# A gated linear attention and a feed-forward layer on one core: wider products of zeros, and another order, engines and banks

## The chip, the cores and the metric

The kernel runs on one core of one Trainium2 chip. The metric is the device time of one execution in microseconds (us); lower is better. A core has five engines, each with its own queue of instructions that it works off in order: TensorE (PE in the profile; its weight loads are shown as PEld), VectorE (DVE), ScalarE (ACT), GpSimd (POOL) and SyncE (SP), which here only issues DMAs. Engines wait for each other by semaphores. TensorE writes its results to eight banks of PSUM; GpSimd does not read these in this kernel.

## What is computed

Per batch and head, a state of 48 x 48 decays and takes in one outer product per time step; a query reads it. The rows that come out, for all heads side by side (384 columns, 3,072 rows), go through two matrix products with a squared ReLU between them.

```python
batch, n_heads, seq, head_dim = (4, 8, 768, 48)
n_tokens, d_model, d_ff = (3072, 384, 2048)
for t in range(S):
    state = alpha[:, :, t, :, None] * state + einsum('bhd,bhe->bhde', k[:, :, t], v[:, :, t])
    y[:, :, t] = einsum('bhd,bhde->bhe', q[:, :, t], state)
h = x @ w_in            # x: y with the heads side by side
r = maximum(h, 0.0)
out = (s * (r * r) + b) @ w_out
```

## The kernel before

The time axis is cut into chunks of 128 steps: 6 chunks for each of 4 batches, 24 blocks in all. Inside a block the recurrence becomes products. The names below are those of the list `ORDER`; the number behind a name is the block, the group or the piece.

- Loads on SP: `pa0` to `pv2` load alpha, q, k, v for two blocks at a time for the first six blocks (384 KB each), `a6` to `v23` for one block (192 KB). `i0` to `i3` load quarters of `w_in` and `o0` to `o3` quarters of `w_out` (768 KB each).
- `ln` (L324, ScalarE) takes the logarithm of alpha, `cum` (L335, L348 to L361, TensorE) sums it along time, `eb`, `ei`, `el` (L368, L373, L381, L386, ScalarE) take exponentials of the sums. `qb` and `kb` (L234, VectorE or GpSimd) multiply q and k by them. `vc` copies v.
- `T` and `Tc` transpose q and k on TensorE and copy the result (the first six blocks); `Td` (L426) does it with a DMA from SP (the others). `A` (L481, L491) gives the scores, `mk` (L502, L508, VectorE) masks them. `KV` (L439, L451), `t` (L464, L466) and `sn` carry the state from block to block. `y`, `ya`, `ys` (L530, L544, L561) give the block's output, transposed, and `ye` copies it to `xd`.
- `m` (L592) is one of 96 pieces of the first matrix product: six products of 256 columns, two blocks at a time (a group of eight `m`). `re` (L599 on ScalarE, L601 on VectorE) is the ReLU out of a bank, `sq` (L609 on ScalarE, L234 on VectorE) the square.
- `w` (L626) is a quarter of the second matrix product for one block: four products of 384 columns. The last block is done in two halves of columns (`w92` to `w95`, L618, eight products of 192). `oe` (L641, L636) adds the bias and scales, `st` (L654, L649) stores.
- `ci`, `co` convert the weights to bf16 on three engines; `ca` to `cd`, `bm`, `be` make the bias row from `w_out`.
- `z` (L659) are products of zeros whose result nobody reads. `FILLS` gives each its bank, the number of products and their width.

There is no loop over the work: `ORDER` is a list written out in full, and L738 to L740 emit it word by word. Each engine gets its instructions in the order in which they stand in it. A prefix (`A:`, `D:`, `P:`) sets another engine than the usual one (`DEF`). The lists `T_BANK`, `C_BANK`, `A_BANK`, `KV_BANK`, `Y_BANK`, `O_BANK`, `H_BANK` name the PSUM bank of each result, and `R_BANK` which of four buffers a ReLU writes. Whoever writes a bank next waits until the last user's result has been read.

Of the kernel before, what the change touches and what calls it, by code (L numbers as in the profile page):

```python
# [29 lines left out]
SB_BANK, BIAS_BANK = 2, 6  # L30
T_BANK = {0: 3, 1: 1, 2: 1, 3: 3, 4: 6, 5: 4}
C_BANK = [0, 4, 6, 5, 4, 5, 2, 2, 5, 1, 4, 4, 7, 6, 0, 1, 2, 5, 7, 4, 0, 5, 2, 3]
A_BANK = [2, 1, 1, 6, 2, 2, 4, 2, 3, 6, 3, 2, 4, 6, 0, 5, 1, 4, 4, 1, 3, 6, 1, 6]
KV_BANK = [5, 0, 0, 3, 5, 0, 2, 3, 2, 0, 6, 0, 0, 7, 5, 2, 1, 0, 7, 3, 2, 4, 4, 0]
Y_BANK = [6, 4, 0, 6, 2, 7, 5, 2, 0, 6, 1, 3, 2, 7, 6, 7, 4, 5, 2, 7, 0, 5, 5, 4]
O_BANK = [0, 3, 4, 7, 0, 6, 1, 5, 1, 3, 4, 3, 6, 3, 0, 6, 6, 3, 3, 5, 4, 7, 5, 2, 1]
# [15 lines left out]
qb2 T1 KV1 pq2 pk2 KV0 P:kb3 zvp3 A:Tc1 el2 z4 A1 ya0 P:kb2 vc2 t0 mk1 t1 z5 T3 ys1 ya1 ln4 ln5 T2
cum5 i3 Tc3 A:vc3 ye1 KV3 KV2 ye0 Tc2 sn1 A3 cum4 eb5 A2 t2 el5 ei5 mk3 ci0 P:ci1 zs2 pv2 i1 ys2
el4 eb4 ei4 sn2 m0 m1 mk2 ys3 t3 P:ci5 re1 ya3 ya2 D:ci4 re0 sq0 qb5 ye3 ye2 m5 qb4 m4 m8 m9 P:ci7
o0 re5 re4 a6 A:sq4 A:sq5 kb5 sq1 re8 T5 kb4 m13 re13 T4 Tc5 ci6 A:sq13 m12 A5 D:re9 Tc4 D:of0 mk5
m7 sn3 m6 A:sq8 vc5 m15 s0 D:vc4 D:re12 A:sq9 o3 A4 re6 re7 ci2 KV5 KV4 m14 mk4 ci3 A:sq12 o1 o2
re15 m2 ya5 a8 a7 a9 k7 k6 A:sq15 ya4 ys4 t4 D:sn4 ys5 q6 D:co1 D:re14 P:co0 D:re2 D:ye4 v6 m10 m3
w0 w8 sm0 sq7 ln6 q7 v7 k8 sq6 A:sq14 re3 ye5 re10 U0 m21 m16 A:sq10 m11 re21 A:sq21 co7 sq2 sq3
ca0 se0 D:re16 P:co6 cum6 D:co3 el6 re11 A:sq11 ei6 ca3 sq16 m23 m18 w12 m17 m19 re18 ln8 D:re23
D:co2 re19 eb6 re17 ln7 ca1 D:co5 w4 D:co4 cb0 w9 m20 ca2 cb1 kb6 sq17 A:sq18 w13 A:sq19 cc0 qb6  # L60
cd0 D:re20 a11 a10 m22 cum8 w10 w1 cum7 w5 w11 w2 ei8 el8 eb7 ln9 el7 re22 qb7 w6 w14 bm0 w3 eb8
w7 ei7 A:sq22 be0 oe0 sq23 D:vc6 A:sq20 A:vc7 Td6 P:kb7 w20 w16 KV6 w15 w21 cum9 oe2 Td7 q8 t6
ln10 ei9 ln11 oe1 oe3 eb9 w22 A6 A7 w17 w18 w23 mk6 cum10 mk7 y6 y7 q9 KV7 oe5 D:ye7 k9 v9 v8 q10
k10 w19 eb10 ei10 ye6 el10 cum11 m31 el9 t7 oe4 P:qb8 m26 P:qb9 D:re31 kb8 A:vc8 ei11 m25 m24
D:re25 D:re24 m27 A:sq25 m29 eb11 A:sq24 P:kb9 D:re26 P:qb10 k11 Td9 D:re27 D:vc9 P:kb10 A:sq31
KV8 m30 w24 q11 Td8 w28 re30 KV9 A:sq26 a12 sq30 D:re29 sn7 t8 D:sn8 A:sq27 m28 w25 re28 A:sq28
A:sq29 A9 Td10 v10 A8 w29 t9 w26 ln12 mk9 v11 a13 w27 w30 mk8 cum12 y8 y9 A10 P:kb11 w31 P:qb11
ye8 oe6 sn9 D:vc10 el12 ye9 ln13 mk10 vc11 eb12 m37 KV10 Td11 m34 oe7 m36 t10 q13 k13 cum13 k12
a15 D:re34 A11 re36 re37 mk11 m35 ei12 el13 sq36 m39 eb13 m32 sn10 re39 ei13 a14 q12 q14 y11 v13
qb13 sq39 sq37 kb12 ye11 y10 P:kb13 D:re35 ln15 ye10 D:re32 A:sq35 m38 m33 m46 cum15 D:re33 A:sq32  # L70
m44 A:sq33 a17 D:re46 ln14 D:re38 sq38 m45 m42 w36 m41 cum14 Td13 A:sq46 sq34 el15 D:re42 D:re44
ln17 m40 A:sq44 P:qb12 Td12 k14 v12 w37 re45 el14 w38 w39 ei14 eb15 ei15 D:re40 A13 D:vc13 sq45
oe9 A12 A:sq40 mk12 v14 w32 mk13 m43 w33 re41 sq41 a18 a16 w34 A:vc12 eb14 re43 P:kb14 KV12 A:sq43
v15 m47 q15 sq42 t12 w35 A:vc14 ln16 y13 y12 qb14 ye12 w44 D:ye13 re47 cum17 v19 k15 cum16 oe8 k16
eb16 A:sq47 ei17 KV13 P:qb15 m53 v16 Td14 t13 w40 m48 kb15 D:re48 eb17 ln18 el16 re53 ei16 KV14
m55 w41 m52 D:re55 m50 Td15 A:sq55 re52 m54 P:kb16 vc15 w45 KV15 m51 D:sn13 A:sq48 re54 q17 D:re50
t14 D:vc19 A14 mk14 sn14 A:sq50 A15 mk15 t15 w42 w46 A:sq52 q18 A:sq54 w47 m49 y14 re51 y15 oe11
k19 k17 P:qb17 vc16 D:re49 D:sn15 KV16 w43 q16 ye14 ye15 m59 a19 A:sq49 ln19 A:sq51 sq53 qb16 k18
a20 a21 q20 P:kb17 cum18 m57 oe10 w52 m61 Td16 re57 D:re59 Td17 m56 w53 m58 q19 v17 A:sq57 ei18
sq59 D:re61 v18 cum19 ei19 el19 el18 eb18 w54 t16 m63 re58 A:sq61 w55 m62 D:re63 D:re56 sn16 eb19  # L80
P:kb18 sq58 P:kb19 q21 a22 A16 A17 mk17 oe13 ln20 w48 w49 cum20 k20 k23 vc17 w50 m60 w51 D:re62
ei20 el20 eb20 A:sq56 mk16 re60 P:qb19 y17 y16 w56 ln21 A:vc18 a23 ye17 ln22 qb18 KV18 cum21 ye16
ei21 P:kb20 t18 KV19 w57 cum22 A:sq63 Td18 eb21 ei22 k21 m67 ln23 eb22 oe12 sq60 P:qb20 Td19 t19
sq62 m71 w60 el21 P:qb21 D:re71 D:re67 m68 m69 el22 m66 w61 A:sq71 kb21 k22 v20 D:re68 re66 w62
P:kb22 A:sq67 A18 A19 A:sq66 D:re69 cum23 w58 w63 Td20 mk19 m64 Td21 q22 sn19 y19 mk18 y18 D:ye18
eb23 ye19 w59 m65 ei23 A:vc20 v22 oe15 oe14 sq69 m72 re65 A21 A20 m70 A:sq65 P:qb22 re64 re72 mk21
mk20 vc22 v21 A:sq64 m76 re70 vc21 m79 KV20 st2 q23 st0 P:kb23 A:sq68 A:sq70 st11 Td22 st8 st3
re79 w64 t20 qb23 sq79 w65 KV21 D:sn20 t21 w66 w67 w68 m77 re76 oe16 re77 A:sq76 w69 sq72 Td23 m74
m78 D:re74 y21 sq77 re78 ye21 y20 sn21 A22 mk22 A:sq78 ye20 A23 KV22 m75 w70 m73 m86 D:re75 mk23
re86 A:sq75 w71 v23 st16 D:re73 m80 m81 st1 oe17 D:vc23 t22 m87 sq86 m85 sn22 re87 y22 y23 A:sq87  # L90
re80 ye23 A:sq80 sq73 sq74 m84 D:ye22 m82 re84 m88 D:re81 m83 A:sq81 st15 st10 re82 sq84 st4 m89
w80 re83 m94 sq82 A:sq83 m91 re85 A:sq85 re94 D:re89 w81 st7 st9 sq94 w76 m90 A:sq89 w72 m92 w77
re92 A:sq92 D:re90 D:re91 A:sq91 A:sq90 m95 w73 w78 D:re88 m93 w82 w74 w75 w79 sq88 D:re95 oe18
# [17 lines left out]
def kernel(  # L111
# [319 lines left out]
    def kv_view(n):  # L431
        return BANK[KV_BANK[n]][:, 0:384].rearrange("a (p e) -> a p e", p=NP)

# [220 lines left out]
        e.dma_start(out=out[n * C : (n + 1) * C, :], in_=out_sb[n % NOS])  # L654

    def o_z(e, x):
        bank, m, w = FILLS[x]
        for _ in range(m):
            nc.tensor.matmul(  # L659
                out=BANK[bank][:, 0:w], lhsT=zeros[:, 0:128], rhs=zeros[:, 0:w], start=True, stop=True  # L660
            )
# [109 lines left out]
```

## Time and profile before

| | us |
|---|---|
| median of 3 runs | 178.99 (178.43 to 179.17) |
| profiled execution, its own time | 179.38 |
| its span, first to last instruction | 177.7 |
| TensorE busy in the span | 169.5 |
| VectorE, ScalarE, GpSimd busy | 134.0, 111.3, 54.6 |
| first product of zeros starts | 1.25 |
| last product ends, end of the span | 174.6, 177.7 |

The durations come from the profiled execution. Its own time is 0.39 us above the median of the runs, and its span is 1.68 us shorter than its own time. Matmuls are pipelined: the duration of a single one is longer than the spacing from one to the next, so a group of products is priced by the spacing of their starts. In the timeline, a bracket behind an instruction gives the idle time of its engine just before it and what ended it; "issue" means that the profile shows no semaphore that ended it.

### The profile page before, as it was taken

How to read it: one execution, taken by the hardware profiler on the slowest of the kernel's cores; microseconds unless marked ns; L12 is line 12 of the kernel's file. 1: busy time of each engine (PE TensorE's matmuls, PEld its weight loads, DVE VectorE, ACT ScalarE, POOL GpSimd, SP SyncE). 2: the span in 40 equal slices, each digit the busy share in tenths (PEclk: the TensorE clock that was granted, in tenths of full speed). 3: DMA queues.
4: the chain of work that ended last, by engine and by line, in shares of the span. 5: the costliest groups of instructions: out<-in, count | busy, mean ns of one | idle time of the engine just before them, and what ended most of it. 6: DMA issues, size and time to landing. Idle time of an engine off the chain costs nothing.

```text
span 177.7 us, 5545 instructions
## 1 busy us (share of the span) xinstructions
PE 169.5 (95%) x2289; PEld 127.7 (72%) x2289; DVE 134.0 (75%) x239; ACT 111.3 (63%) x242; POOL 54.6 (31%) x83
## 2 busy tenths in 40 slices
...
GB/s 146 325 318 289 271 329 360 313 280 199 141 224 191 200 144 198 146 203 174 192 171 226 128 209 184 197 210 186 207 127 266 185 344 139 4 0 0 141 208 98
DMA packets 113708, 34.96 MB, mean 197 GB/s; under 512 B 106900, under 2 KB 112148, under 8 KB 113684
## 3 DMA queue, kind: packets, MB, share of 16 engines
...
q8 instruction: 18, 0.29, 0.7%
...
## 4 chain that ended last, share of the span: by engine, by line
PE 71%; DVE 7%; SPq 7%; ACT 6%; DMA 4%; issue 3%; POOL 1%; DVEq 0%; ACTq 0%
PE bank_ps L626 31%; PE bank_ps L592 28%; SPq L188 5%; DMA wst<-in_moe_w_in_dram 4%; PE bank_ps L481 3%; ACT gt L609 2%; PE bank_ps L544 2%; DVE r L601 2%; ACT r L599 2%; PE bank_ps L335 2%; PE bank_ps L530 2%; SPq L258 2%; PE bank_ps L618 1%; DVE am L502 1%; PE bank_ps L439 1%
## 5 line engine op out<-in xcount | busy, mean ns | idle before, releaser
L592 PE MATMUL bank_ps<-xd,w_in_bf 128*128 128x256 bf16 x576 | 72.0, 273 | 1.8 <-DVE r L601 1.1
L626 PE MATMUL bank_ps<-w_out_bf,gt 128*128 128x384 bf16 x368 | 68.1, 326 | 0.0
L592 PEld LDWEIGHTS <-w_in_bf 128*128 128x128 bf16 x576 | 54.5, 98 | 12.2 <-issue 0.9
L626 PEld LDWEIGHTS <-gt 128*128 128x128 bf16 x368 | 34.5, 98 | 19.5 <-issue 0.2
L599 ACT ACTIVATE r<-bank_ps 128x512 bf16<-128x512 f32 x52 | 30.6, 597 | 16.6 <-PE bank_ps L592 11.9
L609 ACT ACTIVATE gt<-r 128x512 bf16<-128x512 bf16 x61 | 36.8, 628 | 5.4 <-DVE r L601 4.9
L601 DVE TENSOR_SCALAR r<-bank_ps 128x512 bf16<-128x512 f32 x44 | 29.3, 685 | 8.9 <-PE bank_ps L592 6.4
L234 POOL TENSOR_TENSOR qk<-k_in,binv 128x384 bf16<-128x384 f32 x16 | 17.0, 1066 | 39.3 <-ACT binv L373 26.6
L502 DVE TENSOR_TENSOR am<-bank_ps,U_bf 128x1024 bf16<-128x1024 f32 x18 | 21.5, 1220 | 4.1 <-PE bank_ps L481 3.6
L234 DVE TENSOR_TENSOR gt<-r 128x512 bf16<-128x512 bf16 x35 | 17.1, 507 | 3.5 <-ACT r L599 3.3
L641 DVE SCALAR_TENSOR_TENSOR wst<-bank_ps,s_col,bias_w 128x384 f32<-128x384 f32 x23 | 14.0, 614 | 6.9 <-PE bank_ps L626 6.4
L234 POOL TENSOR_TENSOR qk<-q_in,b_s 128x384 bf16<-128x384 f32 x13 | 13.4, 1031 | 17.4 <-DMA q_in<-in_q_dram 13.9
L373 ACT ACTIVATE binv<-bank_ps 128x384 f32<-128x384 f32 x24 | 11.9, 498 | 10.3 <-PE bank_ps L342 7.7
L234 POOL TENSOR_TENSOR s_st<-t,blast 128x384 bf16<-128x384 bf16 x11 | 9.4, 855 | 23.7 <-DVE t L466 23.6
L229 ACT ACTIVATE xd<-bank_ps 128x384 bf16<-128x384 f32 x19 | 9.4, 520 | 9.8 <-PE bank_ps L544 9.2
L324 ACT ACTIVATE la<-a_in 128x384 bf16<-128x384 f32 x24 | 12.3, 522 | 5.1 <-DMA a_in<-in_alpha_dram 5.1
L368 ACT ACTIVATE b_s<-bank_ps 128x384 f32<-128x384 f32 x24 | 12.0, 499 | 4.5 <-PE bank_ps L342 3.4
L466 DVE TENSOR_TENSOR t<-bank_ps,s_st 64x192 bf16<-64x192 f32 x32 | 11.3, 352 | 1.7 <-POOL s_st L234 0.6
L234 DVE TENSOR_TENSOR qk<-q_in,b_s 128x384 bf16<-128x384 f32 x11 | 6.0, 550 | 6.3 <-DMA q_in<-in_q_dram 5.9
L659 PE MATMUL bank_ps<-zeros 128*128 128x128 bf16 x81 | 7.2, 255 | 1.3 <-DVE half_bf L695 1.3
L508 DVE TENSOR_TENSOR am<-bank_ps,maskp 128x1024 bf16<-128x1024 f32 x6 | 7.3, 1223 | 0.7 <-PE bank_ps L491 0.6
L530 PE MATMUL bank_ps<-qkT,s_st 128*32 128x128 bf16 x240 | 6.8, 221 | 0.6 <-issue 0.6
...
## 6 DMA issues: line engine op xcount, KB each, us to landing
...
```

The costliest lines, as they stand in the source:

```text
L234: e.tensor_tensor(out=o, in0=x, in1=y, op=ALU.mult)
L324: e.activation(out=la_sb[u % NLA].rearrange("a (r h) d -> a r h d", r=2)[..., 0:D], in_=seen("a", u), func=AF.Ln,)
L368: e.activation(out=b_sb[u % NB].rearrange("a h d -> a (h d)"), in_=BANK[C_BANK[u]][:, 0:384], func=AF.Exp)
L373: e.activation(out=binv_sb[u % NB].rearrange("a h d -> a (h d)"), in_=BANK[C_BANK[u]][:, 0:384], func=AF.Exp, scale=-1.0,)
L466: e.tensor_tensor(out=t1_sb[n % 2][r, :, c], in0=kv[r, :, c], in1=s_sb[(n - 1) % 3][r, :, c], op=ALU.add,)
L502: e.tensor_tensor(out=am.rearrange("a e p t -> a (e p) t"), in0=a_ps.rearrange("a e p t -> a (e p) t"), in1=U_bf.unsqueeze(1).to_broadcast ...
L592: nc.tensor.matmul(out=hp[:, i * 256 : (i + 1) * 256], lhsT=w_in_bf[:, kk, 128 * j : 128 * (j + 1)], rhs=xd_sb[g % 3][:, kk, :], start=(kk ...
L599: e.activation(out=r_sb[R_BANK[w]], in_=BANK[H_BANK[w]], func=AF.Relu)
L601: e.tensor_scalar_max(r_sb[R_BANK[w]], BANK[H_BANK[w]], 0.0)
L609: e.activation(out=o, in_=r, func=AF.Square)
L626: nc.tensor.matmul(out=BANK[bank][:, 0:d_model], lhsT=gt_sb[:, j, c0 : c0 + C], rhs=w_out_bf[:, j, :], start=(j == 0), stop=(j == NJ - 1),)
L641: e.scalar_tensor_tensor(out=out_sb[n % NOS], in0=BANK[O_BANK[n]][:, 0:d_model], scalar=s_col[:, 0:1], in1=bias_w, op0=ALU.mult, op1=ALU.add,)
```

## The change

The products of zeros are given by columns instead of by number and width, and each takes up to 512 columns. The list `ORDER`, the engines in it and all bank lists are replaced by others. The operations other than `z` are the same; the numbers of engines change thus: `re` from 52 on ScalarE and 44 on VectorE to 67 and 29; `sq` from 61 and 35 to 57 and 39; `ye` from 19 and 5 to 12 and 12; `vc` from 8 on each of ScalarE, VectorE and GpSimd to 6, 2 and 16; `ci` from 4, 1 and 3 to 4, 2 and 2; `co` from 1, 5 and 2 to 3, 4 and 1; `Tc` from 1 and 5 to 2 and 4. The diff, with the bank lists and the middle of the order cut out:

```diff
-FILLS = [(0, 32, 128), (1, 12, 128), (1, 4, 128), (1, 15, 128), (7, 12, 128), (7, 6, 128)]
+FILLS = [(0, 4288), (0, 256), (0, 1280), (0, 256), (2, 2240), (2, 960), (4, 2048), (4, 320), (3, 896)]
...
     def o_z(e, x):
-        bank, m, w = FILLS[x]
-        for _ in range(m):
+        bank, cols = FILLS[x]
+        while cols:
+            w = min(cols, 512)
             nc.tensor.matmul(
                 out=BANK[bank][:, 0:w], lhsT=zeros[:, 0:128], rhs=zeros[:, 0:w], start=True, stop=True
             )
+            cols -= w
```

The start of each engine's queue, before and after:

```
SP before: pa0 pk0 pa1 pq0 pv0 pq1 pk1 pa2 pv1 i0 i2 pq2 pk2 i3 pv2 i1 o0 a6 s0 o3 o1 o2 a8 a7 a9
SP after:  pa0 pa1 pv0 pk0 pq0 pq1 pk1 pa2 pv1 i0 i2 pk2 pq2 i3 pv2 i1 a7 s0 o0 a6 o1 o2 k7 o3 k6
TensorE before: z0 cum0 cum1 z1 cum2 cum3 z2 T0 z3 A0 T1 KV1 KV0 z4 A1 ya0 z5 T3 ys1 ya1 T2 cum5 KV3 KV2
  A3 cum4 A2 ys2 m0 m1 ys3 ya3 ya2 m5 m4 m8 m9 T5 m13 T4 m12 A5 m7 m6 m15 A4 KV5 KV4 m14 m2 ya5 ya4 ys4
TensorE after: z0 cum0 cum1 z1 cum2 z2 cum3 z3 KV1 z4 T0 T1 KV0 z5 A0 z6 T3 A1 ys1 T2 ya0 A3 ya1 KV3 KV2
  ys2 cum5 A2 cum4 m0 ya3 ya2 ys3 m4 m1 m9 m8 m12 z7 T5 m5 T4 m13 A5 A4 z8 m15 m7 m14 KV4 KV5 ya5 ya4 m6
ScalarE before: ln0 ln1 eb0 ei0 ln2 el1 ln3 ei1 el0 eb1 ei2 eb2 vc0 eb3 el3 ei3 Tc1 el2 ln4 ln5 vc3 ye1 ye0 eb5 el5 ei5 ci0
ScalarE after:  ln0 ln1 ln2 el1 ei1 ei0 ln3 eb1 el0 eb2 eb0 eb3 el3 el2 ei2 ei3 Tc1 ln5 Tc3 ln4 vc2 ye0 ye1 ci0 ci1 eb5 ei5
VectorE before: qb0 kb1 zvp0 zvp2 Tc0 vc1 mk0 qb2 t0 mk1 t1 Tc3 Tc2 t2 mk3 mk2 t3 ci4 sq0
VectorE after:  vc1 zqk2 kb1 kb0 qb0 qb1 qb2 Tc0 t0 mk0 t1 mk1 Tc2 mk3 t2 mk2 ci4 t3 ye2
```

The end of TensorE's and SP's queues:

```
TensorE before: w75 w79 w84 w83 w88 w89 w85 w86 w90 w87 w91 w92 w93 w94 w95
TensorE after:  w79 w83 w74 w87 w92 w88 w75 w89 w94 w90 w91 w93 w95
SP before: st18 st19 st12 st6 st17 st20 st14 st21 st22 st23 st24
SP after:  st16 st2 st12 st18 st21 st20 st19 st22 st23 st24
```

More of the change, by code (lines that the diff above doesn't have):

```diff
@@ L29 @@
 TAIL = 1
[L30 to L36, printed above, removed]
@@ L37 @@
-H_BANK = [5, 7, 1, 6, 6, 1, 1, 7, 3, 7, 5, 6, 0, 1, 6, 4, 3, 6, 3, 5, 1, 1, 6, 1, 0, 3, 6, 5, 4,
-7, 0, 5, 5, 0, 4, 4, 5, 0, 2, 1, 4, 2, 4, 3, 5, 6, 4, 4, 0, 0, 6, 7, 2, 1, 1, 7, 6, 2, 2, 5, 4, 4,
-7, 1, 1, 4, 5, 4, 7, 3, 0, 1, 2, 0, 0, 5, 5, 7, 4, 1, 7, 6, 3, 6, 2, 0, 2, 3, 7, 2, 2, 6, 0, 6, 3,
-2]
-R_BANK = [3, 0, 2, 1, 2, 1, 0, 3, 2, 0, 3, 1, 1, 1, 1, 2, 2, 0, 3, 1, 0, 0, 1, 2, 3, 1, 1, 3, 1,
-2, 0, 2, 0, 1, 3, 2, 2, 0, 2, 1, 1, 2, 0, 3, 3, 2, 0, 1, 0, 1, 3, 3, 1, 2, 0, 3, 2, 3, 3, 1, 3, 2,
@@ L43 @@
-1, 0, 1, 2, 2, 1, 3, 0, 0, 3, 2, 0, 3, 1, 1, 0, 1, 1, 2, 0, 2, 0, 1, 0, 2, 2, 0, 3, 1, 2, 3, 3, 1,
-1]
-FILLS = [(0, 32, 128), (1, 12, 128), (1, 4, 128), (1, 15, 128), (7, 12, 128), (7, 6, 128)]
-ORDER = """
-zz0 Us0 P:zqk0 P:zla0 pre0 pa0 Ui0 zt1 sml0 pk0 pa1 ln0 P:zla1 zs1 ln1 zqk2 zvp1 z0 cum0 eb0 ei0
-pq0 cum1 pv0 ln2 el1 ln3 pq1 ei1 pk1 mp0 D:zt0 zqk1 zs0 id0 P:kb0 pa2 qb0 kb1 zvp5 D:zvp0 z1 cum2
-el0 eb1 cum3 P:qb1 z2 T0 pv1 ei2 D:zvp2 Tc0 D:vc1 eb2 A:vc0 eb3 i0 z3 A0 P:qb3 i2 mk0 zvp4 el3 ei3
@@ L52 @@
[L52 to L93, printed above, removed]
@@ L94 @@
-w84 w83 st13 oe19 w88 re93 sq93 w89 w85 A:sq95 oe20 st5 w86 w90 w87 st18 st19 w91 st12 st6 st17
-oe21 st20 st14 oe22 st21 st22 w92 w93 oe23 st23 w94 w95 oe24 st24
+SB_BANK, BIAS_BANK = 5, 7
+T_BANK = {0: 6, 1: 3, 2: 5, 3: 6, 4: 7, 5: 1}
+C_BANK = [4, 5, 7, 1, 2, 0, 1, 3, 5, 1, 1, 3, 2, 1, 3, 5, 1, 2, 7, 1, 4, 3, 2, 4]
+A_BANK = [1, 2, 6, 6, 4, 0, 4, 2, 3, 6, 4, 2, 2, 0, 1, 5, 2, 5, 4, 0, 3, 6, 2, 6]
+KV_BANK = [0, 5, 1, 5, 3, 0, 7, 7, 1, 6, 7, 0, 1, 0, 2, 1, 0, 0, 5, 7, 5, 5, 4, 0]
+Y_BANK = [0, 4, 3, 4, 1, 5, 5, 3, 2, 3, 7, 3, 3, 0, 2, 5, 4, 3, 1, 0, 2, 5, 5, 7]
@@ new lines @@
+O_BANK = [4, 3, 0, 2, 0, 6, 0, 5, 7, 6, 4, 3, 0, 5, 6, 3, 0, 1, 3, 1, 7, 4, 0, 2, 6]
+H_BANK = [1, 5, 4, 0, 7, 2, 2, 6, 7, 0, 3, 7, 6, 6, 0, 7, 3, 6, 7, 1, 5, 7, 2, 6, 5, 1, 7, 4, 6,
+2, 0, 3, 7, 3, 0, 1, 6, 1, 5, 5, 2, 4, 1, 2, 4, 3, 6, 0, 3, 6, 5, 0, 4, 4, 6, 6, 5, 7, 7, 4, 3, 6,
+2, 2, 0, 5, 2, 7, 1, 5, 4, 4, 7, 0, 0, 2, 1, 2, 6, 0, 3, 5, 5, 4, 2, 0, 3, 2, 5, 0, 6, 3, 2, 2, 6,
+5]
+R_BANK = [2, 0, 0, 0, 0, 2, 3, 2, 2, 3, 0, 1, 1, 3, 2, 1, 2, 2, 3, 1, 0, 1, 3, 3, 2, 0, 2, 3, 3,
+0, 1, 3, 2, 1, 3, 0, 1, 0, 1, 2, 3, 3, 2, 0, 1, 0, 2, 3, 1, 1, 2, 1, 2, 3, 0, 0, 3, 2, 1, 2, 0, 1,
@@ new lines @@
+0, 3, 0, 3, 3, 1, 3, 0, 2, 1, 0, 2, 1, 2, 0, 3, 0, 3, 2, 2, 0, 2, 3, 0, 2, 1, 1, 0, 0, 0, 3, 3, 1,
+2]
+FILLS = [(0, 4288), (0, 256), (0, 1280), (0, 256), (2, 2240), (2, 960), (4, 2048), (4, 320), (3, 896)]
+ORDER = """
+zz0 zqk1 D:zvp3 D:zvp2 D:zs1 D:zs0 zvp1 Ui0 P:zqk0 P:zla1 D:zt1 zla0 pre0 of0 zvp5 sml0 D:zs2 pa0
+pa1 D:zvp0 id0 ln0 pv0 pk0 Us0 mp0 pq0 ln1 pq1 D:vc1 zqk2 z0 cum0 cum1 vc0 ln2 pk1 el1 ei1 ei0 ln3
+eb1 el0 z1 cum2 kb1 pa2 pv1 z2 cum3 z3 KV1 eb2 eb0 kb0 i0 qb0 z4 T0 qb1 qb2 Tc0 eb3 el3 el2 ei2
@@ new lines @@
+ei3 T1 KV0 i2 P:qb3 pk2 t0 z5 A0 P:kb3 mk0 A:Tc1 z6 T3 t1 ln5 A:Tc3 A1 mk1 P:kb2 vc3 ys1 zt0 sn1
+T2 ln4 ya0 A3 ya1 A:vc2 pq2 ye0 Tc2 KV3 KV2 ys2 mk3 ye1 t2 cum5 sn2 zvp4 A2 cum4 ci0 m0 ya3 i3 mk2
+ci1 eb5 D:ci4 ya2 ys3 pv2 t3 ei5 el5 ei4 D:ye2 ye3 m4 kb4 re0 re4 kb5 m1 m9 sq4 m8 eb4 qb5 m12 el4
+A:sq0 qb4 z7 T5 re1 P:ci5 i1 re8 sq8 m5 T4 P:ci6 sn3 Tc5 U0 vc5 re12 re9 A:sq9 m13 A5 Tc4 mk5 A4
+ci7 re13 z8 m15 re5 m7 mk4 sq12 A:sq5 sq13 A:vc4 re7 m14 a7 s0 KV4 o0 a6 KV5 A:sq7 re15 ci3 ya5
+re14 ya4 D:ci2 m6 m2 t4 ln7 A:sq14 D:sn4 A:sq15 m10 o1 ys5 ys4 m3 D:re6 sq1 re10 o2 D:ye4 D:ye5
@@ new lines @@
+ln6 A:sq10 m11 A:sq6 m22 m16 re16 re22 A:sq22 A:sq16 D:re11 sq11 sm0 k7 D:re3 se0 o3 P:co1 m18 m19
+sq3 D:co0 m17 D:co3 k6 re2 cum7 a8 q6 D:re19 ca0 sq2 co2 el7 re18 w12 w8 w0 cum6 a9 q7 v6 ca1 sq19
+sq18 m21 eb7 v7 a11 m20 w13 el6 D:co4 w1 ei6 co5 re17 w9 re20 eb6 re21 ei7 ca2 cb0 kb6 w14 kb7
+D:co6 qb6 m23 w4 w2 A:sq17 A:sq21 co7 Td6 a10 ca3 cb1 qb7 re23 ln8 A:sq20 cc0 ln9 w5 w20 w15 w10
+cum8 Td7 k8 A:vc7 q8 w11 cum9 k9 ln11 v8 cd0 a12 w6 q9 vc6 bm0 eb8 ei9 w7 w3 w21 be0 KV6 ln10 eb9
+el8 el9 ei8 w22 cum10 eb10 A:sq23 oe3 ei10 oe2 oe1 A7 oe0 A6 t6 w16 w17 w18 w23 mk6 mk7 y7 y6 w19
@@ new lines @@
+k10 P:kb9 P:qb8 P:kb8 KV7 ye6 P:qb9 q10 v9 q11 D:ye7 ln12 el10 m24 cum11 m27 t7 oe5 re24 ei11 m25
+oe4 m26 m28 vc8 Td8 re27 Td9 eb11 D:re25 k11 A:sq24 sq27 KV8 m29 a13 re28 m31 m30 A:sq25 D:re26
+v11 v10 sn7 re29 A:sq26 cum12 sq28 w28 P:kb10 re30 qb10 t8 re31 A:sq29 sq30 D:sn8 w29 A8 A9 eb12
+el12 ei12 w30 vc9 A:sq31 v13 ln13 P:kb11 P:qb11 vc11 vc10 w24 w25 mk8 Td10 mk9 v12 y8 y9 KV9 cum13
+ye9 w26 Td11 D:ye8 KV10 t9 w31 w27 oe7 sn9 m33 oe6 D:re33 v16 q12 t10 m36 a14 el13 ei13 eb13 k13
+m35 A10 A11 m34 A:vc13 mk10 D:re34 mk11 A:sq33 sn10 re36 re35 m32 re32 A:sq32 sq35 m37 m38 y10 q13
```

26 lines of the change are left out of this document (added).

## The prediction

> **What bounds the kernel now.** I read the page's first and fourth parts, then two stretches, then TensorE's timeline.
>
> ```profile
> PE 169.5 (95%) x2289; PEld 127.7 (72%) x2289; DVE 134.0 (75%) x239; ACT 111.3 (63%) x242; POOL 54.6 (31%) x83
> ...
> PE 71%; DVE 7%; SPq 7%; ACT 6%; DMA 4%; issue 3%; POOL 1%; DVEq 0%; ACTq 0%
> ```
>
> TensorE is busy 95% of the span and carries 71% of the chain that ended last. The chain's other shares lie where TensorE waits, mostly at the start:
>
> ```profile
> 0.00:22.08 22.08, 18.59 (x428) 15.60 (x428) 13.47 (x32) 14.58 (x37) 15.49 (x37) 1.00 0.96 270
> 22.08:177.70 155.62, 150.90 (x1862) 112.07 (x1862) 120.53 (x208) 96.76 (x207) 39.10 (x46) 1.00 0.87 186
> ```
>
> (Columns: length; busy time of PE, PEld, DVE, ACT, POOL; clock; DMA share; GB/s.) Up to 22.08 us the DMA engines are full (0.96) and TensorE waits for inputs and weights, with products of zeros between. From 22.08 to its last product at 174.55, 152.5 us, it is nearly never idle. I priced each step there by the start-to-start spacing usual for its kind (an m of six products 0.65 us, a w of four 0.65, and so on): 147.4 us. So 5.1 us are stalls, and no order can save more than that after 22.08. The large ones, in TensorE's timeline (the bracket is idle time and what ended it):
>
> ```profile
> 20.36 0.35 PE L530 MATMUL bank_ps<-qkT,s_st 128*32 128x128 bf16 x12 [0.57 <-issue]
> 20.64 0.81 PE L561 MATMUL bank_ps<-am,vp 64*32 64x128 bf16 x64
> 22.08 1.16 PE L592 MATMUL bank_ps<-xd,w_in_bf 128*128 128x256 bf16 x9 [0.62 <-POOL w_in_bf L231]
> ...
> 34.40 0.82 PE L592 MATMUL bank_ps<-xd,w_in_bf 128*128 128x256 bf16 x6 [0.74 <-DVE r L601]
> ...
> 73.02 0.41 PE L544 MATMUL bank_ps<-am,vp 128*32 128x128 bf16 x16 [0.43 <-DVE am L502]
> ...
> 82.39 0.83 PE L592 MATMUL bank_ps<-xd,w_in_bf 128*128 128x256 bf16 x6 [0.39 <-DVE r L601]
> ```
>
> Over the usual spacing the last three cost 0.91, 0.60 and 0.56 us; all three end with VectorE. The first (ys3) ends with "issue": all its semaphores had come by 19.8. I read it as missing instructions. The DMA part has the records:
>
> ```profile
> q8 instruction: 18, 0.29, 0.7%
> ```
>
> That is 16 KB, some 256 instructions, a packet (4,578 weight loads and products in 18). Their starts, 11.10, 17.90, 21.41, 29.06, 35.30, 44.66 and so on, fit requests at instructions 200, 456, 712, 968 (+256): I read that packet n+1 is asked for as packet n is entered, and must be there 256 instructions later. Instruction 456 is ya1, 14.1 us; its packet began at 17.90, after 3.8 us, ended at 18.87, and ys3, at instruction 702 to 726, ran at 20.36, 1.5 us on. The same packets delay loads: of each load's 16 landings the last is 1.3 us behind the fifteenth for pa2 and pv1 (14.00, 15.17; packet of 11.10) and 1.1 us for i2 (20.89; packet of 17.90). ScalarE pays at once:
>
> ```profile
> 14.08 0.94 ACT L324 ACTIVATE la<-a_in 128x384 bf16<-128x384 f32 x2 [2.00 <-DMA a_in<-in_alpha_dram]
> ```
>
> **The change, part by part. Wider products.**
>
> ```profile
> L659 PE MATMUL bank_ps<-zeros 128*128 128x128 bf16 x81 | 7.2, 255 | 1.3 <-DVE half_bf L695 1.3
> ```
>
> 81 products of 128 columns (10,368 columns) become 28 (12,544). z0 goes from 4,096 to 4,288 columns at 0.111 us per 128 (32 in 3.55 us): +0.17, ending at 4.97. That moves cum0, but kb0 and qb0 wait for pk0 and pq0, which now land later than that: nothing. z1 to z6 hold 7,040 columns against 6,272 in z1 to z5, at 0.056 us per 128: +0.34, all in waits for loads. z7 and z8 are new, 1,216 columns, 0.53 us, behind m12 and A4: nothing if TensorE waits there for w_in anyway, 0.53 if not. I take +0.25.
>
> **Instruction packets.** 53 products and 53 weight loads less put every later step 106 instructions earlier in the count. Counting the new order: 200 falls in z6 (was A0), 456 in KV3 (was ya1), 712 in ys3 again, 968 in ya5 (was A5); 17 packets instead of 18.
>
> **Start.** SP's order is now pa0 pa1 pv0 pk0 pq0 pq1 pk1 pa2 pv1 i0 i2: the same bytes ahead of i0, one pair per 1.21 us, so pk0 lands at 7.9 (was 5.4) and pq0 at 9.05 (was 7.9). qb0 waits for both pq0 and eb0, T0 starts near 10.0 (was 8.57): +1.4. The chain behind it: Tc0 0.69, A0 0.4, mk0 1.2, t1 0.7, mk1 1.2 on VectorE bring ya1 to 16.0 (was 14.2). If the first packet, now asked for at 12.0 to 12.9, runs behind pa2 and pv1, these land at 12.7 and 13.9, 1.3 us earlier, and ln4, ln5, vc2, vc3 with them. On ScalarE vc2, ye0, ye1, ci0 (0.63, 0.52, 0.52, 0.85) then end near 18.3, so m0 starts at 18.4 (was 18.31). There was slack: xd was ready at 16.7, and m0 waited for i0 (17.2) and ci0. ya3, ya2 and ys3 are past at 20.5; m4 waits for i2 and ci4 (0.69): 20.5 with i2 at 19.8, 21.6 with i2 at 20.9. Before, m5 came at 22.08 with m1 (0.65) already done. So 21.2 to 22.3 stands against 22.08: −0.9 to +0.2 with the packets in time, up to +3 if not (first rival). I take −0.2.
>
> **The dense stretch.** ReLU (re) moves from VectorE to ScalarE 15 times (44 to 29 by 0.685; 52 to 67 by 0.597), 7 ye and 4 sq the other way, vc to GpSimd. By the rows VectorE has about 7 us less to do, ScalarE 4 more: 127 and 116. In the old order VectorE's queue was long where the stalls are. Banks: I summed TensorE's work between one user of a bank and the next, after its first 20 us. Under 1.2 us there were 8 such returns, now 4; under 1.6 us 35, now 23. From an m to the first w that needs it, 10 were under 3.5 us, now 3. If stalls went with the 35 and 23, 5.1 would become 3.4, −1.7; if the new order only moves them, 0; several queues on ScalarE at 0.6 to 0.9 each could add 2. I take −1.2, nearer the count.
>
> **Tail.** The last five w are as dense as before. But st18, st21, st20 and st19 now follow w75, which ends 3.9 us before the last product, and st22, st23, st24 come right behind: five stores of 192 KB and two of 96 KB, 1.18 MB. Eight stores issued from 142.2 to 146.2 us ran at 344 GB/s (the page's GB/s in that slice), so 3.4 us, nearly hidden: 0 to +0.5, I take +0.1.
>
> **Sum.** 0.25 − 0.2 − 1.2 + 0.1 = −1.05. The profiled execution took 179.38 (span 177.7 and 1.68 around it): 178.33. The median, 178.99, lies 0.39 below it, so 177.9.
>
> **Rivals.**
>
> - Late packets, slower, 0.20. If the first packet waits 3.8 us, as that of 17.90 did behind 2 KB pieces of i0 and i2, it starts at 15.8 to 16.7 and serves at 18.2 to 19.1; KV3, ready near 16.2, stands 2 to 3 us, and m0 with it. The second packet, asked for only then, holds ys3 again. m4 starts at 23.5 to 24.5; with m1 undone, +2 to +3. With +0.25, −1.2 and +0.1: 180.1 to 181.1. It decides at a start after 13.7 us for the first packet (KV3's 16.2 less 0.96 and 1.5). For: the 3.8 us. Against: the packet of 11.10 waited 1.2 to 2.5 us and that of 21.41 waited 1.0; with such waits the first packet starts at 13.0 to 15.4, and the worst of that holds KV3 by 1.7 us, of which the wait for i2 behind m0 hides about 1. [...]
> - ScalarE becomes the queue, slower, 0.10. From 70 to 80 us of TensorE's work its rows sum to 11.9 us. A relu late there holds a bank as VectorE's did: three or four stalls of 0.6 to 0.9 above the old 5.1, +2.4 in place of −1.2, and hence +2.5: 181.5 at most, 180.3 with half. Against: before and after that stretch it has 5.8 and 4.4.
> - The change does not do what it says, 0.24: packets collide as before and the stalls only move. −0.2 to +0.5, 178.8 to 179.5.
> - All of it works, 0.06: the start gives −0.9 and stalls fall to 2 us (−3.1): with +0.25 and +0.1, about 175.3; half of that, 177.1.
>
> My forecast has 0.40. About 0.5% (0.9 us) is what a measurement of this kernel can tell from no change. Faster, below 178.1: 0.40 + 0.06 = 0.46; same 0.24; slower, above 179.9: 0.20 + 0.10 = 0.30. The range leaves out the best corner and the worst of the slow cases: 176.4 to 180.6; the forecast alone has 177.0 to 178.1.
>
> **What would show it.** Right: pa2 and pv1 landing near 12.7 and 13.9; no "issue" idle before KV3 or ys3; m4 at 20.5 to 21.6; above-spacing time after the start near 4 us, few "DVE r" releasers; last landing under 0.5 us later after the last product than the 3.1 of now. Wrong: "issue" idle over 1 us before KV3 or ys3, or "ACT r" as releaser of TensorE in the dense stretch for over 2 us.

## The result and the profile after

The kernel after takes 189.41 us (median of 4 runs, 188.93 to 190.72), beside 178.71 of the kernel before on the same chip: ratio 1.0608, 95% interval 1.0549 to 1.0668. It is 6.1% slower; forecast were 177.9 us, with a range to 180.6. The profiled execution took 189.42 us, its span is 187.7, ten more than before. From its page, the busy times, the chain that ended last and the queue of instruction packets:

```profile
PE 171.4 (91%) x2233; PEld 124.5 (66%) x2236; DVE 129.1 (69%) x231; ACT 115.3 (61%) x247; POOL 55.7 (30%) x86
...
q8 instruction: 17, 0.28, 0.6%
...
PE 58%; SPq 17%; DMA 12%; issue 5%; POOL 4%; DVE 2%; POOLq 0%
```

VectorE and ScalarE have nearly the work that was forecast (127 and 116). But TensorE's share of the chain falls from 71% to 58%, and the shares of SP's queue and of the DMA rise from 7 and 4 to 17 and 12. The same two stretches, up to 22.08 us and behind it, now of the kernel after and in the same columns:

```profile
0.00:22.08 22.08, 18.21 (x349) 11.49 (x352) 14.22 (x37) 13.73 (x31) 11.32 (x32) 1.00 0.99 292
22.08:187.70 165.62, 153.18 (x1884) 113.04 (x1884) 114.83 (x195) 101.59 (x216) 44.38 (x54) 1.00 0.82 172
```

Most of the loss lies behind 22.08. By the prediction's usual spacings TensorE's time above the work (products of zeros not counted as work) is 22.4 us from its first product to its last, instead of 12.5: +9.9 (the last product ends at 184.43, before at 174.55). TensorE's timeline shows where:

```profile
17.79 0.23 PE L561 MATMUL bank_ps<-am,vp 64*32 64x128 bf16 x2 [1.83 <-issue]
...
22.34 0.23 PE L561 MATMUL bank_ps<-am,vp 64*32 64x128 bf16 x2 [0.82 <-issue]
...
79.49 0.40 PE L481 MATMUL bank_ps<-qkT 64*128 64x128 bf16 x8 [0.76 <-DMA qkT<-qk]
...
93.79 0.40 PE L481 MATMUL bank_ps<-qkT 64*128 64x128 bf16 x8 [0.99 <-DMA qkT<-qk]
...
108.10 0.40 PE L481 MATMUL bank_ps<-qkT 64*128 64x128 bf16 x8 [1.23 <-DMA qkT<-qk]
...
123.73 0.49 PE L592 MATMUL bank_ps<-xd,w_in_bf 128*128 128x256 bf16 x3 [1.51 <-ACT blast L386]
...
133.35 0.40 PE L481 MATMUL bank_ps<-qkT 64*128 64x128 bf16 x8 [1.07 <-DMA qkT<-qk]
```

The first two stand just ahead of KV3 and ys3; I read them as the late instruction packets: from the one stop to the other there are 128 products with as many weight loads, 256 instructions, as the prediction counts for a packet. The others are new: A11, A12, A14 and A18 (the last line) wait for a `Td`, and A19 right behind A18 does too. Above the usual spacing A11, A12, A14, A18 and A19 cost 0.88, 1.15, 1.35, 1.24 and 1.32 us; KV14 costs 1.13 (it waits for `vc`), m59 1.62. The stalls of before that ended with VectorE are gone. The view of waits (us in all, times, longest) has GpSimd, before and then after, and SP after:

```profile
POOL vp L231 <- DMA v_in<-in_v_dram: 2.9, 3, 1.7
...
POOL vp L231 <- DMA v_in<-in_v_dram: 31.2, 6, 17.5
...
SPq L261 <- DVE w_in_bf L231: 8.2, 1, 8.2
```

GpSimd stands 31.2 us at `vc` for a late v, with the rest of its queue behind it. At m59 this is the chain: vc19 waits 9.69 us for v19; behind it stand qb19, vc17 and sn16; `el20` on ScalarE waits for sn16, and m59 writes the bank that `el20` reads. SP stands at o1 from 25.2 to 33.7 us, 8.2 us by the profile: o1 overwrites the buffer that ci2 and ci3 read, and in the new order these end at 33.4 (on VectorE, which the view names) and 33.7 (on ScalarE). In the kernel before, SP stood 3.7 us there, with o3 sent just ahead. In the kernel after the DMA engines run nearly dry meanwhile. 28 to 36 us, before and then after:

```profile
28.00:36.00 8.00, 7.26 (x156) 5.50 (x155) 7.73 (x13) 6.87 (x13) 2.28 (x4) 1.00 1.04 329
```

```profile
28.00:36.00 8.00, 7.84 (x179) 6.31 (x178) 7.42 (x12) 7.55 (x16) 0.99 (x1) 1.00 0.43 95
```

Some 4.9 us of transfers are lost there (0.61 of 8 us). From 40 to 140 us the share is about 1 in both kernels. So two theories stood against each other, though both can be true at once: **lag** (the transfers never make up for the time lost at 28 to 36 us) and **order** (the new queues want their transfers sooner, whatever the start).

### The profile page after: what moved, and what is told of

It reads as the page before. It is cut to its first block, busy times and chain, and to the rows that moved or that the text cites. A ratio compares the mean times of both kernels' runs of the same rounds, so it can differ in the third digit from the quotient of the medians.

```text
span 187.7 us, 5431 instructions
## 1 busy us (share of the span) xinstructions
PE 171.4 (91%) x2233; PEld 124.5 (66%) x2236; DVE 129.1 (69%) x231; ACT 115.3 (61%) x247; POOL 55.7 (30%) x86
## 4 chain that ended last, share of the span: by engine, by line
PE 58%; SPq 17%; DMA 12%; issue 5%; POOL 4%; DVE 2%; POOLq 0%
PE bank_ps L592 21%; PE bank_ps L626 18%; SPq L172 13%; DMA qkT<-qk 5%; DMA v_in<-in_v_dram 5%; SPq L426 4%; PE bank_ps L660 4%; POOL qk L234 2%; DMA k_in<-in_k_dram 2%; PE bank_ps L530 2%; PE bank_ps L417 2%; POOL vp L231 2%; PE bank_ps L561 2%; PE bank_ps L618 1%; DVE am L502 1%
## 5 line engine op out<-in xcount | busy, mean ns | idle before, releaser
L592 PE MATMUL bank_ps<-xd,w_in_bf 128*128 128x256 bf16 x576 | 70.8, 273 | 1.8 <-ACT blast L386 1.5
L599 ACT ACTIVATE r<-bank_ps 128x512 bf16<-128x512 f32 x67 | 38.7, 597 | 25.4 <-PE bank_ps L592 20.4
L609 ACT ACTIVATE gt<-r 128x512 bf16<-128x512 bf16 x57 | 34.5, 632 | 1.3 <-DVE r L601 0.9
L601 DVE TENSOR_SCALAR r<-bank_ps 128x512 bf16<-128x512 f32 x29 | 19.8, 688 | 12.0 <-PE bank_ps L592 9.6
L234 DVE TENSOR_TENSOR gt<-r 128x512 bf16<-128x512 bf16 x39 | 20.0, 527 | 4.6 <-ACT r L599 4.2
L641 DVE SCALAR_TENSOR_TENSOR wst<-bank_ps,s_col,bias_w 128x384 f32<-128x384 f32 x23 | 13.7, 613 | 8.5 <-PE bank_ps L626 8.2
L231 POOL CAST vp<-v_in 128x384 bf16<-128x384 f32 (+1 forms) x19 | 9.8, 529 | 31.3 <-DMA v_in<-in_v_dram 31.2
L231 DVE CAST xd<-bank_ps 128x384 bf16<-128x384 f32 x12 | 6.6, 564 | 6.9 <-PE bank_ps L544 6.7
L481 PE MATMUL bank_ps<-qkT 64*128 64x128 bf16 x144 | 6.1, 218 | 5.3 <-DMA qkT<-qk 5.3
L229 ACT ACTIVATE xd<-bank_ps 128x384 bf16<-128x384 f32 x12 | 5.9, 516 | 7.8 <-PE bank_ps L544 4.0
L660 PE MATMUL bank_ps<-zeros 128*128 128x512 bf16 (+5 forms) x25 | 8.0, 439 | 1.6 <-DVE zeros L702 1.3
```

The lines of the kernel that those rows point to most:

```text
L231: e.tensor_copy(out=o, in_=i)
L234: e.tensor_tensor(out=o, in0=x, in1=y, op=ALU.mult)
L592: nc.tensor.matmul(out=hp[:, i * 256 : (i + 1) * 256], lhsT=w_in_bf[:, kk, 128 * j : 128 * (j + 1)], rhs=xd_sb[g % 3][:, kk, :], start=(kk ...
L599: e.activation(out=r_sb[R_BANK[w]], in_=BANK[H_BANK[w]], func=AF.Relu)
L601: e.tensor_scalar_max(r_sb[R_BANK[w]], BANK[H_BANK[w]], 0.0)
L609: e.activation(out=o, in_=r, func=AF.Square)
```

## The experiments

**Instruction packets.** Products of zeros of 128 columns in the kernel after, of up to 512 in the kernel before:

```diff
-            w = min(cols, 512)
+            w = min(cols, 128)
```

> The changed kernel with its products of zeros cut to 128 columns again (98 products instead of 28); order, engines and banks of the change. Theory 'late packets': the two idle times of TensorE that end with issue before KV3 (2.2 us) and ys3 (1.2 us) go, because the requests at instructions 200 and 456 come 100 or more instructions of work earlier; m0 starts near 18 instead of 19.98, ci3 and with it o1 come 2 us earlier (o1 issued near 31.5 instead of 33.7), and 185 to 187 us come out. Theory 'SP's order': at most the 1 us that the start itself gives, 188 to 189.5, and the DMA share from 30 to 40 us stays near 0.57. Theory 'engines': 189.

> The kernel before with its products of zeros, of the same number of columns, given as products of up to 512 columns (22 instead of 81); nothing else changed. Theory 'late packets': the requests come 118 instructions of work later here too, idle time that ends with issue grows from 0.6 to 2 us or more near KV3 to ys3, 180 to 182 us. Theories 'SP's order' and 'engines': 178.3 to 179.2.

The first gave 190.54 us (186.83 to 191.62), the second 178.77, ratio 0.9991 (0.996 to 1.0022). The packets only change places. With 128 columns KV3 runs at once, m0 starts at 18.45 instead of 19.98, and the next packet, asked for in ya0 at about 15, started at 18.82 and ended at 19.78, and stops m0 in its middle:

```profile
18.45 0.49 PE L592 MATMUL bank_ps<-xd,w_in_bf 128*128 128x256 bf16 x3
21.16 0.49 PE L592 MATMUL bank_ps<-xd,w_in_bf 128*128 128x256 bf16 x3 [2.23 <-issue]
```

In a_w128 65 more products of zeros stand ahead of m0, and the stop comes 65 products earlier than that of 22.34 in after. In three of the four runs the mean granted clock was 0.97 to 0.98 (in the profiled one 0.76 from 20 to 27 us, behind this stop, and 0.72 from 134 to 140 us); the one at 1.00 took 186.83, 2.6 us under the kernel after. One run does not settle what the width is worth there. In the kernel before, wider products put the idle time (1.42 us, "issue") into ya2 and change nothing in sum.

**SP's stand at o1.** In the kernel after, o3, k7, k6 and a8 go ahead of o1; in the kernel before, ci3 goes behind sq15 and o3 goes behind o1 and o2, so that SP stands at o1 to 33.6 us, as in after:

```
a_o3    SP: ... a7 s0 o0 a6 o3 k7 k6 a8 o1 o2 q6 a9     (after: a7 s0 o0 a6 o1 o2 k7 o3 k6 a8 q6 a9)
b_idle  SP: ... o0 a6 s0 o1 o2 o3 a8 a7 a9 k7 k6        (before: o0 a6 s0 o3 o1 o2 a8 a7 a9 k7 k6)
```

> The changed kernel with four loads (o3, k7, k6, a8) moved ahead of o1 in SP's queue, so that SP has something to send while o1 waits for ci3. Theory 'the transfers are the second bound, and SP's order starves them': the DMA share from 30 to 40 us rises from 0.57 to over 0.85, the waits of A for its transposed q and k (6.4 us in all) shrink by 3 to 4 us, 185 to 186.5 us. Theory 'late packets alone': the idle time of DMA is a consequence that costs nothing by itself, 189. Theory 'engines': 189.

> The kernel before with ci3 moved behind sq15 on ScalarE and o3 moved behind o2 on SP, so that SP stands at o1 until 34 us with nothing ahead of it, as in the changed kernel. Theory 'the transfers are the second bound': 2 to 3 us of DMA time are lost between 30 and 40 us; with no slack behind them 181 to 182, with a slack of 2 us or more 178.7 to 179.5 although the share falls. Theory 'engines': 178.7 to 179.2, and the share may fall without any effect.

a_o3: 187.82 (186.85 to 189.37), ratio 1.0497 (1.0419 to 1.0576), 1.6 us less than after. The windows show the hole filled and a new one behind it, where SP stands 2.9 us at Td6; the stops at A14, A19, m59 and KV14 stay as they were, that at A18 goes and those at A11 and A12 shrink:

```profile
28.00:36.00 8.00, 8.00 (x182) 6.34 (x180) 7.36 (x13) 7.63 (x15) 0.98 (x1) 1.00 1.00 252
40.00:50.00 10.00, 10.00 (x78) 6.89 (x77) 9.73 (x16) 9.58 (x22) 0.79 (x1) 1.00 0.76 176
```

b_idle: 185.21, ratio 1.0317 (1.0239 to 1.0395). It has the same hole (share 0.42 at 28 to 36 us), but it loses in one place, not along the way. TensorE, and then ScalarE:

```profile
44.63 1.49 PE L591 MATMUL bank_ps<-xd,w_in_bf 128*128 128x256 bf16 x12 [3.86 <-ACT r L598]
46.16 2.72 PE L625 MATMUL bank_ps<-w_out_bf,gt 128*128 128x384 bf16 x8
...
43.19 0.84 ACT L228 ACTIVATE w_out_bf<-wst 128x768 bf16<-128x768 f32 x1 [4.66 <-DMA wst<-in_moe_w_out_dram]
```

ScalarE stands at co7 for o3, the quarter of `w_out` that the edit sent last (it landed at 43.17, in before at 34.99); the ReLU that m17 waits for is behind it. After the stop TensorE is at about half speed (eight products of 384 columns take 2.72 us instead of 1.46; the mean granted clock of the run is 0.989). So most of these 6.2 us are the price of a late weight, and they say little of the hole. Behind that, all the A's together wait 0.4 us.

**SP's order alone.** Each kernel with the other's SP queue (v12, v18 and st1 in a_sp, a17 and v19 in b_sp a few places earlier than there):

> The changed kernel, with SP's queue alone put into the order of the kernel before (three of its 137 DMAs stand elsewhere, v12, v18 and st1, because this order of the engines needs them sooner); all other queues, engines and banks are the change's. Theory 'SP's order': the transposes land at the times of before from Td8 on (within 2 us), the waits of A for them (6.4 us) and of vc for v fall by two thirds, and 182 to 184 us are left, the rest being the start. Theory 'late packets': the transposes are late because the start is, so 187 to 189. Theory 'engines, banks and TensorE's order': 188 to 189.5.

> The kernel before, with SP's queue alone put into the order of the change (a17 and v19 a little sooner); all else as before. Theory 'SP's order': Td9 to Td13 land 4 to 8 us later than in the kernel before, A waits for them, 184 to 188 us. Theory 'late packets': the start of this one has 81 narrow products and its packets in time, so 178.5 to 180. Theory 'engines, banks and TensorE's order': 178.5 to 180.

a_sp took 228.65 us (ratio 1.2739), b_sp 202.20 (1.13), with stops of TensorE of 2 to 8 us; in a_sp GpSimd stands 47.4 us at `vc` for a v and ScalarE 25.7 at `ln` for an alpha. Neither SP order is the bad one: it fits its own kernel's queues, and a queue cannot be changed alone.

**Half the bytes.** Loads from block 6 on bring four of the eight heads (the kernels leave out the other four from there on):

```diff
-                out=flat(x, n).rearrange("a (h d) -> a h d", h=H),
-                in_=SRC[x][b, :, c * C : (c + 1) * C, :].rearrange("h s d -> s h d"),
+                out=flat(x, n).rearrange("a (h d) -> a h d", h=H)[:, 0 : H // 2],
+                in_=SRC[x][b, 0 : H // 2, c * C : (c + 1) * C, :].rearrange("h s d -> s h d"),
```

> The changed kernel with the loads of alpha, q, k and v from block 6 on cut to the first four of eight heads, so half the bytes; it leaves out the other half of these inputs. Every queue has the same instructions in the same order. Theory 'the transfers are the second bound': nothing after the start waits for a load or a transpose for more than 1 us in all, 180 to 182 us, which is the start's loss. Theory 'engines, banks and TensorE's order': TensorE's stalls stay, 187 or more.

> The kernel before with the same halved loads. Theory 'the transfers are the second bound': they were nearly hidden here, 177.5 to 179; how far it falls below 178.9 is what they cost it. Theory 'engines, banks and TensorE's order': the same.

> The changed kernel with halved loads (half of alpha, q, k, v from block 6 on left out) and its products of zeros cut to 128 columns: transfers do not bound it, and the requests for instruction packets come earlier. Theory 'late packets': of the 1.3 us that the halved kernel still loses to the kernel before, the idle time before KV3 goes, and 177.5 to 179.5 come out against 180.27. Theory 'the packets only change places': the wait moves to ya3, as in the 128-column kernel with full loads, 180 to 181.

The kernel after falls to 180.27 us (ratio 1.0093, 1.0058 to 1.0129), that of before stays, 179.46 (1.0054, 1.0022 to 1.0086). So the transfers cost the kernel after 9.1 of its 10.7 us and that of before nothing. 90 to 140 us in the kernel after and then in a_half:

```profile
90.00:140.00 50.00, 43.03 (x572) 30.59 (x570) 33.17 (x58) 29.57 (x68) 18.84 (x22) 1.00 1.08 198
```

```profile
90.00:140.00 50.00, 49.54 (x648) 36.72 (x646) 40.88 (x71) 33.11 (x75) 20.23 (x25) 1.00 0.64 143
```

All stops of A's are gone; the late packets ahead of KV3 and ys3 stay, and with 128-column products besides (180.37) they only move. The start is thus worth some 1.3 us (0.8 against the halved kernel before), and the width nothing once the transfers do not bind.

**Lag or order.** First, eight early loads halved in the kernel after (blocks 6 and 7), and four or eight idle loads ahead of o1 in the kernel before:

```
a_lag           nh = H // 2 if n < 8 else H
b_lag, b_lag8   SP: ... s0 o3 x0 x1 x2 x3 (x4 x5 x6 x7) o1 o2 a8 ...    (x: 192 KB of q into a buffer of its own)
```

> The kernel after, with the eight loads of blocks 6 and 7 alone cut to the first four of their eight heads (the results of those blocks are then wrong in the other heads): at about 1.03 us of the DMA engines per whole load, 4.1 us of transfers are taken out early, about the 4 us that the engines stood idle at 28 to 36 us. All later transfers are whole, and in the same order. If the early idle time alone makes the loss (lag), most of the 9.1 us that halving all later loads gave back comes back: 180 to 183. If the later order of the queues needs its transfers sooner than they can come, whatever the start (order), 186 or more, with the stalls of A14, A18 and A19 still over 0.8 us each.

> The kernel before, with four more loads of 192 KB on SP just ahead of o1, into buffers that nobody reads: about 4.1 us of transfers more, at the place where the kernel after loses as much. Lag: the kernel before then loses what the kernel after did, +6 to +9, 185 to 188, with idle time of A's behind DMA. Order: the order of before takes the lag with less, 0 to +4, 179 to 183.

> The same with eight such loads, about 8.2 us of transfers more. Lag: the time grows with the lag once the slack is gone, so about 4 above the run with four, 189 to 192. Order: the slack of before is some us more than in after; 4 us above the run with four as well if that one was already late, less if it was not.

a_lag took 186.06 us (184.57 to 189.49), b_lag 183.13 (180.58 to 184.88), b_lag8 186.44. They do not decide. a_lag's profile is of the run of 189.49: the late packet left TensorE idle for 2.2 us ahead of ys3, SP stood at o1 to 36.0 and the transfers lost all that they had won. Two other runs, 184.57 and 184.83, are 4.8 and 4.6 us under the kernel after, which lies between the two forecasts; of these there is no profile. In b_lag the lag comes out as one stop at the weights of w9, after which transfers and TensorE are in step again:

```profile
45.88 1.44 PE L634 MATMUL bank_ps<-w_out_bf,gt 128*128 128x384 bf16 x4 [3.49 <-DVE w_out_bf L239]
```

So three more: blocks 6 to 11 halved in after (12 us of transfers, no lag can be left behind them), and the idle loads of before put behind o2, where the weights do not wait:

```
a_half12            nh = H // 2 if n < 12 else H
b_late4, b_late8    SP: ... s0 o3 o1 o2 x0 x1 x2 x3 (x4 x5 x6 x7) a8 a7 a9 k7 k6 ...
```

> The kernel after, with the loads of blocks 6 to 11 alone cut to the first four of their eight heads (the results of those blocks are then wrong in the other heads): about 12 us of transfers less, three times the DMA time that the engines stood idle at 28 to 36 us, and all transfers from block 12 on whole. Lag: the transfers are ahead by block 12, so the stalls of A12, A14, A18 and A19 go too and 180 to 182 is left. Order: the later order falls behind again by itself; A14, A18 and A19 keep over 2 us together and 183 to 185 is left.

> The kernel before, with the four loads more on SP behind o2 instead of ahead of o1, so that the weights are not later and only the blocks' own transfers lag by 4.1 us. Order (before has some 2 us more room, and asks less of its transfers later): 179 to 182, with under 2 us of idle time behind DMA. Lag: 184 to 188, with stalls of A's behind DMA as in after.

> The same with eight loads, 8.2 us of lag. Both theories expect idle time here; order: one or two stops early that the rest then follows, 183 to 187; lag: stops spread to the end as in after, 188 to 192.

b_late4 decides against a lag alone: the kernel before takes a lag of 4.1 us for 1.1 (179.79, ratio 1.0066, 1.004 to 1.0092), and the one large stop in its profile that is new is this, behind a `ln` of ScalarE that waits 2.86 us for a late alpha:

```profile
45.51 0.71 PE L600 MATMUL bank_ps<-xd,w_in_bf 128*128 128x256 bf16 x5 [1.44 <-ACT r L607]
```

Its Td12 lands at 87.3 us (before 86.7), its Td22 at 138.5 (141.4): the transfers catch up. b_late8 has one stop too, at the same m22, of 6.18 us (the `ln` waits 7.61), and the granted clock is 0.77 from 50 to 60 us: 186.23, ratio 1.0433 (1.0389 to 1.0476); no A waits. a_half12 took 183.27 us (181.59 to 184.77), ratio 1.0237 (1.0172 to 1.0302). A11 to A14 and KV14 wait no more, but A18, A19 and m59 do, though the transfers are not behind: SP itself had stood for `qb` or `kb` at Td6, Td8, Td10 and Td13, 7.7 us in all.

The lines of m59, A18 and A19:

```profile
117.98 0.82 PE L593 MATMUL bank_ps<-xd,w_in_bf 128*128 128x256 bf16 x6 [1.30 <-ACT blast L387]
...
126.95 0.40 PE L482 MATMUL bank_ps<-qkT 64*128 64x128 bf16 x8 [0.43 <-DMA qkT<-qk]
128.64 0.40 PE L482 MATMUL bank_ps<-qkT 64*128 64x128 bf16 x8 [1.29 <-DMA qkT<-qk]
```

Of the 9.1 us, 6.1 go with the loads of blocks 6 to 11, and 3.0 stay although no lag is left: these are the later order's own, with the lower clock behind its stops (0.60 from 129 to 133 us, behind those of A18 and A19; the one run with a mean of 1.00, 181.59, leaves 1.3). How the 6.1 divide between the hole at o1 and the order of blocks 6 to 11 is not shown. Filling the hole gave 1.6 and opened another, the same lag in before costs 1.1, and a_lag gave up to 4.8. That a lag costs more in the order with less room fits these figures, but no run tests it by itself.

**What "order" is, counted.** For each `Td`, the loads ahead of it on SP (without the 20 of weights and pairs at the start), and the priced TensorE work ahead of its A (products of zeros left out). "Room lost" is an estimate from these two. Where the work comes no later and four loads more are ahead, at 1.03 us each (192 KB at about 190 GB/s, by the rows of this case), the A has 4.1 us less room:

| | loads ahead of Td, before / after | work ahead of A, before / after, us | room lost, us | cost in after, us |
|---|---|---|---|---|
| A11 | 26 / 28 | 59.4 / 59.4 | 2.1 | 0.88 |
| A12 | 35 / 39 | 71.0 / 72.1 | 2.9 | 1.15 |
| A14 | 46 / 50 | 84.0 / 83.6 | 4.5 | 1.35 |
| A16 | 56 / 57 | 96.4 / 96.6 | 0.8 | 0 |
| A18 | 64 / 67 | 108.5 / 105.3 | 6.3 | 1.24 |
| A19 | 65 / 68 | 108.8 / 105.5 | 6.3 | 1.32 |
| A20 | 67 / 70 | 114.0 / 114.6 | 2.5 | 0 |
| A22 | 71 / 71 | 123.2 / 122.1 | 1.1 | 0 |

The stops are where most room is lost (A20, with 2.5 and no stop, is the exception), and each stop gives room to those behind it (0.88, 1.15, 1.13 at KV14 and 1.35 make 4.5 us by A14). The two others are the same with v: v14 has 43 loads ahead of it (before 37), v19 has 57 (before 42).

**Sorted by need.** The loads and `Td` of after's SP queue sorted by when TensorE needs them; and this queue and that of a_o3 with 128-column products:

```
a_edf  SP: ... a7 s0 a6 o0 o2 k6 k7 o3 o1 q6 a8 a9 q7 v7 a11 v6 a10 k8 q8 Td6 k9 Td7 ...
```

> The changed kernel with SP's queue, from o0 on, sorted by when its own engines' queues need each load or transpose (earliest need first among those whose buffer is free); other queues as in the change. Theory 'the order of the loads and transposes': transposes land 3 to 6 us earlier, 182 to 186 us. Theory 'the start puts the transfers behind': only the moved o3, k6, k7 act, 187 to 189.

> The same sorted queue with 128-column products of zeros. If start and order both count, 180 to 183.5; if only one of them does, the time of the kernel that has it.

> The changed kernel with both edits to its start: 128-column products, and o3, k7, k6, a8 ahead of o1 on SP. Theory 'the start puts the transfers behind': both gains add up, 183 to 185.5 us. Theory 'the order of the loads and transposes behind the start': at most the 1.6 us of the moved loads alone, 186.5 to 188.

a_edf took 190.67 us (ratio 1.0724, 1.0611 to 1.0838), a_edf_w 190.09 (185.35 to 192.34) and a_o3w 189.63 (187.02 to 190.71): nothing gained in the median, though single runs of the last two are 2 to 4 us under the kernel after. But a_edf tries the table, since its counts are others: Td12 has 42 loads ahead (after 39), Td14 53 (50), Td18 and Td19 64 and 65 as in before. From its timeline:

```profile
93.94 0.62 PE L480 MATMUL bank_ps<-qkT 64*128 64x128 bf16 x16 [1.66 <-DMA qkT<-qk]
...
109.34 0.61 PE L480 MATMUL bank_ps<-qkT 64*128 64x128 bf16 x8 [3.45 <-DMA qkT<-qk]
...
133.94 0.62 PE L480 MATMUL bank_ps<-qkT 64*128 64x128 bf16 x16
```

A12 waits 1.82 us above the spacing instead of 1.15, A14 3.57 instead of 1.35, and A18 and A19 (the last line, 16 products without a bracket) not at all. They are reached some 1.7 us later than in after, but Td18 is also issued 4.7 us sooner (122.45 instead of 127.16). The sort puts 15 stores ahead of Td23 (after: 9), and A23, which did not wait in after, then waits 1.71 us: the loads alone do not tell all. The table is thus borne out by four A's, not proved. A kernel that has after's order with only these `Td` moved up was not tried. No kernel here beats both; b_w512 equals the kernel before.

## Why the prediction was wrong, point by point

- **Fills, +0.25.** No run times this term by itself; 128 or 512 columns made no difference in the kernel before or with halved loads.
- **Start, −0.2.** m4 starts at 22.78, where before m5 came at 22.08; forecast were 20.5 to 21.6. pa2 and pv1 landed at 12.75 and 13.95 (forecast 12.7, 13.9), i2 at 19.5. By the prediction's count of instructions the packet was asked for at 11.97, as forecast, and it ran at 15.59, past the 13.7 from which the late-packet rival decides; KV3 stood 1.8 us by the row, where that rival had 2 to 3, and the next packet, asked for at 17.95, held ys3. The rival was right in its mechanism and too high in its price: it had m4 later by 2 to 3, the halved kernel shows 1.3 in all, since m4 would have waited for i2 for part of it. In before I had counted waits of 1.0 to 2.5 us and one of 3.8; in after they are 3.6, 2.1 and 3.8 us by that count, with the DMA share at 1.06 to 1.11 meanwhile (packets of 15.59, 20.06, 26.34), so the share gives no price here.
- **Dense stretch, −1.2: this step failed.** Its reason was right as far as it went: VectorE's queue and the banks were eased, and the stalls of m3, y9 and m46 went. But I priced the new order by the engines' rows and by the banks only. On SP's queue I counted up to i2 and no further, though each `Td` and v that an A or a `vc` waits for stands in it. Counting the loads ahead of each `Td` in the two lists needs no run: it gives 3 or 4 more for nine of the twelve from Td10 to Td21 and would have shown A14, A18 and A19 at 4 to 6 us less room, beside the 1.2 us that I took as won. In place of −1.2 stand +9.1, waits for transfers that the term put at nothing.
- **"No order can save more" than 5.1 us** bounded the gain. I set no such bound on the loss; "several queues on ScalarE" at +2 was the worst that I had for this stretch, and it did not come: no ReLU of ScalarE held TensorE for more than 0.4 us; at m59 ScalarE itself waited for GpSimd.
- **Tail, +0.1.** Right: from the last product to the end of the span 3.3 us, before 3.15.
- **The rivals.** All had TensorE, ScalarE or the start in view; none had the transfers of the dense stretch. I had read the DMA share of about 1 to 140 us and used it for the start alone.
